# Gated attention and two expert products on one core: the gate applied as a square at the output, routing rows carrying logits and square sums

## The chip, the cores and the metric

The program runs on one NeuronCore of a Trainium2 chip. The metric is the device time of one execution in microseconds. Engines are named as in the profile: PE (TensorE, matrix products), PEld (its weight loads), DVE (VectorE), ACT (ScalarE), POOL (GpSimd) and SP (SyncE, which issues most DMAs). Each engine runs its own instructions in order; semaphores connect them.

## The reference

Three parts run one after the other, all in 32-bit floats:

```python
# 1. gated linear attention, 4 batches x 8 heads x 768 steps x 48 dims
f = sigmoid(f_logit)
for t in range(768):
    state = f[t][:, None] * state + outer(k[t], v[t])
    y[t] = q[t] @ state
x = y as 3072 tokens x 384
# 2. one of 8 experts for each token
logits = (x / |x|) @ (emb / |emb|).T / tau
e = argmax(logits); gate = softmax(logits)[e]
x = gate * (relu(x @ w1[e]) @ w2[e])          # 384 -> 1024 -> 384
# 3. a gated product for all tokens
out = ((x @ w_a) * (x @ w_b)) @ w_out         # 384 -> 1536 -> 384
```

The gate is a positive number for each token. Part 3 is quadratic in `x`, so a factor on a token's `x` comes out of it as its square.

## The kernel before

**Attention (about 0 to 150 us).** 24 groups: 6 chunks of 128 steps by 4 batches. The main loop over `g` issues the instructions of several groups in an order written by hand: `scan_b(g + 2)` and `scan_r(g + 2)` are the products of the gates as scans on VectorE (L197, L208); `scores(g + 1)` (L251) multiplies the scaled keys `kt`, made on GpSimd (L200), with the scaled queries `qc` (L216, VectorE); the masks follow (`mask_a` on ScalarE and GpSimd, `mask_v` on VectorE); `inter` and `intra` make the output, which `turn_y` (L316) turns to tokens by a product with `pick`. That product also gives each token's eight logits, because `pick` carries the expert embeddings divided by norm and `tau`. The norms are made in `names()` (L594 to L605), three pieces run in groups 0 and 1, with a power 0.5 on GpSimd (L599).

**Routing.** `ROUNDS` lists the groups at which a round closes: rounds of 8, 7, 3, 3 and 3 groups. `route` (L360) is a generator that the loop advances with `tick`: the norm of each token by a power on GpSimd (L373), maximum and one-hot on VectorE, ranks by small products on TensorE, a tanh on ScalarE for the exponentials, the softmax denominator `den` (L415 to L421), and the slot number `posi` (L412). `scatter_row` (L432) then writes 128 rows of 388 floats to `slots` in DRAM: 4 columns of head (number and denominator) and 384 of `x`. Each scatter is an indirect DMA on GpSimd's queue.

**The early half of expert 0.** At group 21 `early_load` reads the first 224 rows of expert 0, `early_gate` makes the rate (reciprocal of the denominator) and scales the rows by it on ScalarE (L460), `early_turn` turns them on TensorE (L467). `early_h`, `early_split` and `early_y` compute them while the last rounds are routed. Overflow flags and offsets follow on VectorE (L750 to L766).

**Experts (about 180 to 430 us).** 64 steps, 8 for each expert, 448 rows an expert. `rows_load` (L876) reads an expert's rows into the one buffer `rows`; `rows_rate` and `rows_gate` (L886, L892) scale them by the gate in place, on ScalarE (L896) after a rate on VectorE (L889, L890); `x_turn` (L915) turns them on TensorE and splits them in a high and a low part for products of full precision. Each step makes a hidden block (L932 to L934), splits it (`hh` on ScalarE L955, `hl` on VectorE L956) and multiplies it with the second weights (L989). `y_part` copies the finished expert into `yT` by ScalarE and VectorE (L1007, L1005). Loaded weights are split in two parts by `job_run` (L814): experts' weights in one ScalarE conversion (L817) and three subtractions (L820), the third part's weights, which are 64-bit words, by a longer VectorE chain (L828 to L838). `ids_store` keeps the token numbers in `idlist` in DRAM, in the order in which the rows stand in `yT`.

**Gated product (about 430 to 884 us).** 6 tiles of 512 tokens by 12 steps. `ab_part` makes the two products and multiplies them (L1088, L1092), splits the result in `gh` and `gl` (L1093, L1094), and `q_mm` multiplies with `w_out`, one step later. In the first ten steps the last wide weights are still split. `q_out` (L1111) copies 128 tokens of the result out and scatters them to the output by `idx`, made at L1057 from the list `idr` (L1050).

## Time and profile before

| | us |
|---|---|
| median of 3 runs | 891.82 (891.37 to 892.36) |
| profiled execution | 893.16 |
| its span | 891.4 |
| PE busy | 840.3 (94%) |
| DVE busy | 426.6 (48%) |
| ACT busy | 355.9 (40%) |
| POOL busy | 248.4 (28%) |

The span is what the profile covers; the profiled execution's own time holds 1.8 us more. Busy shares are means over stages with different limits. Matmuls overlap, so that a busy PE is not necessarily at its peak.

### The profile page before, as it was taken

What the parts mean: (1) busy time and instruction counts of PE and PEld (TensorE: products, weight loads), DVE (VectorE), ACT (ScalarE), POOL (GpSimd) and SP (SyncE); (2) the same over time, 40 slices, a digit from 0 to 9 for tenths busy, and PEclk for the clock granted to TensorE, in tenths of its full rate; (3) what the DMA queues carried; (4) which work ended last, traced back from release to release, by engine and by line L of the source; (5) the groups of instructions that cost most, each with busy time, mean ns of one, the idle gap of its engine ahead of it and who ended that gap; (6) DMA issues with size and microseconds to landing.
All of it is one profiled execution on the core that took longest, in us unless ns stands there. A gap on an engine that the chain in (4) does not pass through costs nothing. (4 is left out here: it accounts for less than half of the span.)

```text
span 891.4 us, 12984 instructions
## 1 busy us (share of the span) xinstructions
PE 840.3 (94%) x5149; PEld 742.5 (83%) x5149; DVE 426.6 (48%) x719; ACT 355.9 (40%) x681; POOL 248.4 (28%) x235
## 2 busy tenths in 40 slices
PE   6898987886999999999998999999999999999996
PEld 4787876875988898899887888888888888888885
DVE  8999995434354345447688523221322312222221
ACT  4798974343455445544443222121222212212111
POOL 6446865432634443461222110010010001001001
PEclk8899998988999999999999999999999999999998
DMA  9888851343534544442333000000000000000001
GB/s 188 207 213 204 242 161 71 111 133 102 174 111 145 198 141 138 139 145 73 103 107 107 1 36 1 1 36 0 1 27 10 1 1 35 1 1 36 1 1 39
DMA packets 35592, 76.60 MB, mean 86 GB/s; under 512 B 4604, under 2 KB 17428, under 8 KB 35524
## 3 DMA queue, kind: packets, MB, share of 16 engines
q1 hardware_dynamic: 32324, 65.91, 26.4%
q0 software_dynamic: 3072, 9.49, 2.9%
q8 instruction: 42, 0.69, 0.3%
q10 hardware_dynamic: 128, 0.30, 0.1%
q14 instruction: 26, 0.21, 0.1%
HBM read 63.79 MB, written 11.90 MB: 85 GB/s over the span
## 5 line engine op out<-in xcount | busy, mean ns | idle before, releaser
L934 PE MATMUL pa<-a,w 128*128 128x512 f32 (+1 forms) x438 | 170.7, 390 | 0.0
L933 PE MATMUL pa<-a,w 128*128 128x512 f32 (+1 forms) x438 | 170.5, 389 | 0.0
L932 PE MATMUL pa<-a,w 128*128 128x512 f32 (+1 forms) x438 | 169.2, 386 | 0.0
L1092 DVE TENSOR_TENSOR rows<-rows,pa 128x512 f32<-128x512 f32 (+1 forms) x73 | 49.6, 679 | 242.7 <-PE pa L934 242.7
L1119 POOL DMA_INDIRECT out<-yT,idx x24 | 23.5, 980 | 363.7 <-ACT yT L1117 358.2
L1088 ACT ACTIVATE rows<-pa 128x512 f32<-128x512 f32 (+1 forms) x73 | 43.1, 591 | 164.7 <-PE pa L934 164.4
L1093 ACT ACTIVATE gh<-rows 128x512 fp32r<-128x512 f32 (+1 forms) x73 | 45.6, 625 | 143.9 <-DVE rows L1092 143.9
L1107 PE MATMUL pq<-w,gl 128*128 128x384 f32 x288 | 97.6, 339 | 2.8 <-DVE gl L1094 2.6
L820 POOL TENSOR_TENSOR w<-raw,w 128x512 fp32r<-128x512 f32 x56 | 84.8, 1535 | 55.2 <-ACT w L817 50.7
L1105 PE MATMUL pq<-w,gh 128*128 128x384 f32 x288 | 97.2, 337 | 0.8 <-ACT gh L1093 0.8
L1106 PE MATMUL pq<-w,gh 128*128 128x384 f32 x288 | 96.9, 337 | 0.4 <-POOL w L838 0.4
L989 PE MATMUL po<-hh,w 128*128 128x448 f32 (+1 forms) x384 | 89.7, 365 | 6.9 <-ACT yT L1007 5.7
L934 PEld LDWEIGHTS pa<-a,w 128*128 128x128 f32 x438 | 82.3, 188 | 16.8
L933 PEld LDWEIGHTS pa<-a,w 128*128 128x128 f32 x438 | 82.3, 188 | 15.3
L932 PEld LDWEIGHTS pa<-a,w 128*128 128x128 f32 x438 | 82.4, 188 | 15.0
L1094 DVE TENSOR_TENSOR gl<-rows,gh 128x512 fp32r<-128x512 f32 (+1 forms) x73 | 60.0, 822 | 52.1 <-ACT gh L1093 52.1
L989 PEld LDWEIGHTS po<-hh,w 128*128 128x128 f32 x384 | 68.2, 191 | 15.0 <-ACT yT L1007 9.6
L838 POOL TENSOR_TENSOR w<-raw,w 128x768 fp32r<-128x768 f32 x18 | 33.9, 1881 | 144.0 <-ACT w L837 138.7
L955 ACT ACTIVATE hh<-ph 128x448 fp32r<-128x448 f32 (+1 forms) x64 | 33.3, 520 | 101.3 <-PE ph L934 101.2
L932 PE MATMUL ph<-a,w 128*128 128x448 f32 (+1 forms) x192 | 69.8, 363 | 0.1
L956 DVE SCALAR_TENSOR_TENSOR hl<-ph,hh 128x448 fp32r<-128x448 f32 (+1 forms) x64 | 38.0, 593 | 66.0 <-ACT hh L955 65.8
L933 PE MATMUL ph<-a,w 128*128 128x448 f32 (+1 forms) x192 | 69.3, 361 | 0.0
(202 smaller groups left out, 1432.9 us busy)
## 6 DMA issues: line engine op xcount, KB each, us to landing
raw<-moe_w SPq DMA_DIRECT2D x32, 768.0 KB, 4.7
qkf<-qkf SPq DMA_DIRECT2D x44, 288.0 KB, 6.0
rows<-slots SPq DMA_DIRECT2D x7, 679.0 KB, 6.6
vx<-vx SPq DMA_DIRECT2D x24, 192.0 KB, 4.1
raw<-moe_w_a SPq DMA_DIRECT2D x6, 768.0 KB, 4.4
raw<-moe_w_b SPq DMA_DIRECT2D x6, 768.0 KB, 4.7
raw<-moe_w_out SPq DMA_DIRECT2D x6, 768.0 KB, 4.3
slots<-raw SPq DMA_DIRECT2D x8, 291.0 KB, 4.3
```

What stands on the lines that cost most here:

```text
L820: (G if i < NPOOL else V).tensor_tensor(out=wt[:, 1, f], in0=raw[:, f], in1=wt[:, 0, f].bitcast(F32), op=ALU.subtract)
L932: T.matmul(out=out, lhsT=wh, rhs=xh, start=first, stop=False)
L933: T.matmul(out=out, lhsT=wl, rhs=xh, start=False, stop=False)
L934: T.matmul(out=out, lhsT=wh, rhs=xl, start=False, stop=last)
L989: T.matmul(out=OS[e][k], lhsT=w[:, j % 4, k * 128:(k + 1) * 128], rhs=x, start=(j == 0 and w is wh and x is hh), stop=(j == FJ - 1 and x i ...
L1088: A.activation(out=ab[:, r], in_=pa, func=ACTF.Copy)
L1092: V.tensor_tensor(out=ab[:, r], in0=ab[:, r], in1=pp[1], op=ALU.mult)
L1093: A.activation(out=gh[:, r], in_=ab[:, r], func=ACTF.Copy)
L1094: V.tensor_tensor(out=gl[:, r], in0=ab[:, r], in1=gh[:, r].bitcast(F32), op=ALU.subtract)
L1105: T.matmul(out=q, lhsT=gh[:, c], rhs=wh[:, f % 4], start=(f == 0), stop=False)
L1106: T.matmul(out=q, lhsT=gh[:, c], rhs=wl[:, f % 4], start=False, stop=False)
L1107: T.matmul(out=q, lhsT=gl[:, c], rhs=wh[:, f % 4], start=False, stop=(f == F2J - 1))
```

## The change

Rows are scattered ungated. Their head grows from 4 to 10 columns (`XO`, `RW`): token number, square sum, eight logits. ScalarE's square accumulates straight into the row, and the logits are reduced straight into it. `route` keeps only what the slot number needs. The token numbers of all groups are written once. The heads of an expert's rows go to `heads` in DRAM instead of the numbers to `idlist`; at step `IDS` they are read back with a token on each partition (`idf`), and in steps 1 to 6 of the gated product `gates` makes the square of the gate for all 3072 tokens at once. `q_out` multiplies by it.

Beside that: the rows of expert 1 have a buffer of their own (`rows1`, the tail of `yT[2]`) and are loaded with those of expert 0, those of expert 2 at step 0; the turning of rows stands in steps 3 to 5 for every expert; rounds are of 8, 6, 4, 3 and 3 groups; two scatters a group; the early load is at group 22; the embedding norms are made ahead of the loop; the conversions of weights 4 to 7 are cut in thirds over three steps. The core of the diff:

```diff
-ROUNDS = (7, 14, 17, 20, 23)
+ROUNDS = (7, 13, 17, 20, 23)
...
         def route(rd):
             nb = rd["n"]
-            lg, ssq = rd["lg"][:, 0:nb], rd["ssq"][:, 0:nb]
+            lg = rd["xb"][:, 0:nb, 2:XO]
...
-            nrm = rt("nrm", 1)
-            G.tensor_tensor(out=nrm[:, :, 0], in0=ssq, in1=half[:, 0:nb], op=ALU.pow)
-            G.tensor_scalar(out=nrm, in0=nrm, scalar1=1e-6, scalar2=None, op0=ALU.add)
-            yield
...
-            V.reciprocal(out=nrm, in_=nrm)
-            yield
-            V.tensor_tensor(out=z, in0=z, in1=bc(nrm), op=ALU.mult)
...
-            A.activation(out=z, in_=z, func=ACTF.Tanh, scale=0.5)
...
-            den = rt("den")
-            V.tensor_scalar(out=den, in0=z, scalar1=-1.0, scalar2=1.0, op0=ALU.mult, op1=ALU.add)
-            yield
-            V.reciprocal(out=den, in_=den)
-            yield
-            V.scalar_tensor_tensor(out=den, in0=z, scalar=1.0, in1=den, op0=ALU.add, op1=ALU.mult)
-            yield
-            V.tensor_reduce(out=rd["xb"][:, 0:nb, 1:2], in_=den, axis=AX.X, op=ALU.add)
...
+        en_ps = ps_r.tile([128, NE], F32, tag="r", name="en_ps")
+        A.activation(out=esq, in_=emb[0:HP], func=ACTF.Square)
...
         scores(0)
+        for p in range(NP):
+            T.matmul(out=en_ps, lhsT=onesf, rhs=esq[:, p], start=(p == 0), stop=(p == NP - 1))
+        A.activation(out=en, in_=en_ps, func=ACTF.Copy)
         turn_k(0)
         scan_b(1)
+        G.tensor_tensor(out=en, in0=en, in1=half[:, 0:NE], op=ALU.pow)
+        G.tensor_scalar(out=en, in0=en, scalar1=1e-6, scalar2=tau, op0=ALU.add, op1=ALU.mult)
...
-            if g == 21:
+            if g == 22:
                 early_load()
...
-            for _ in range(2 if g < 18 else 3):
+            for _ in range(2):
                 scatter_row()
...
             if g == 22:
-                early_gate()
                 w_lo(V, 2)
...
             if g in (20, 23):
-                for _ in range(3):
+                for _ in range(3 if g > 20 else 2):
                     scatter_row()
...
+        rows1 = yT[2][:, NT - 4 * RW:NT].rearrange("p (j w) -> p j w", j=4)
+        rows_of = lambda e: rows1 if e == 1 else rows
...
+            if c is None and n < 8:
+                for i in range(3):
+                    f = slice(i * 512, (i + 1) * 512)
+                    A.activation(out=wt[:, 0, f], in_=raw[:, f], func=ACTF.Copy)
+                    (G if i < NPOOL else V).tensor_tensor(out=wt[:, 1, f], in0=raw[:, f], in1=wt[:, 0, f].bitcast(F32),
+                                                          op=ALU.subtract)
+                    if i < 2:
+                        yield
+                return
...
             if s == 0:
-                rows_rate(0)
-                rows_gate(0, 2, V)
-                rows_gate(0, 3)
...
         rows_load(0)
+        rows_load(1)
         while wstate["load"] < 6:
             w_load()
...
             if s == 0:
                 ids_copy(0)
-                rows_load(1)
+                rows_load(2)
                 ids_store(0)
-            if j == late:
-                rows_rate(e + 1)
-            if late <= j < late + 2:
-                rows_gate(e + 1, 2 * (j - late))
-                rows_gate(e + 1, 2 * (j - late) + 1)
             w_more(s)
-            if late + 2 <= j < late + 5:
-                x_turn(e + 1, j - late - 2)
-            if j == late + 4:
+            if 3 <= j <= 5:
+                x_turn(e + 1, j - 3)
+            if j == 5:
                 ids_copy(e + 1)
-                rows_load(e + 2)
+                if e > 0:
+                    rows_load(e + 2)
...
             if s == IDS:
-                SP.dma_start(out=idr, in_=idlist[0, 0:NT].rearrange("(a b) -> a b", a=24))
+                SP.dma_start(out=idf, in_=heads[0:NT].rearrange("(t p) w -> p t w", p=128))
...
+        def gates():
+            nt = NT // 128
+            bc = lambda t: t.unsqueeze(2).to_broadcast([128, nt, NE])
+            lg = idf[:, :, 2:XO]
+            z, den, nrm, mx = gz[:, 0], gz[:, 1], gm[:, 0], gm[:, 1]
+            G.tensor_tensor(out=nrm, in0=idf[:, :, 1], in1=half, op=ALU.pow)
+            V.tensor_reduce(out=mx, in_=lg, axis=AX.X, op=ALU.max)
+            V.tensor_tensor(out=z, in0=lg, in1=bc(mx), op=ALU.subtract)
+            yield
+            yield
+            V.tensor_scalar(out=nrm, in0=nrm, scalar1=1e-6, scalar2=None, op0=ALU.add)
+            V.reciprocal(out=nrm, in_=nrm)
+            V.tensor_tensor(out=z, in0=z, in1=bc(nrm), op=ALU.mult)
+            A.activation(out=z, in_=z, func=ACTF.Tanh, scale=0.5)
+            yield
+            V.tensor_scalar(out=den, in0=z, scalar1=-1.0, scalar2=1.0, op0=ALU.mult, op1=ALU.add)
+            V.reciprocal(out=den, in_=den)
+            yield
+            V.scalar_tensor_tensor(out=den, in0=z, scalar=1.0, in1=den, op0=ALU.add, op1=ALU.mult)
+            V.tensor_reduce(out=g2, in_=den, axis=AX.X, op=ALU.add)
+            V.tensor_scalar(out=g2, in0=g2, scalar1=1e-9, scalar2=None, op0=ALU.add)
+            yield
+            V.reciprocal(out=g2, in_=g2)
+            V.tensor_tensor(out=g2, in0=g2, in1=g2, op=ALU.mult)
+            yield
...
             if i % 2:
-                V.tensor_copy(ob, QS[tt][i])
+                V.tensor_scalar(out=ob, in0=QS[tt][i], scalar1=sq, scalar2=None, op0=ALU.mult)
             else:
-                A.activation(out=ob, in_=QS[tt][i], func=ACTF.Copy)
+                A.activation(out=ob, in_=QS[tt][i], func=ACTF.Copy, scale=sq)
...
             q_part(s - 1)
+            if 1 <= s <= 6:
+                next(gate_ops)
             w_start(NE * FJ + s, 1)
```

## Rows read from the trace of the kernel before

**Rows 1.** Busy us by stage: span, PE, PEld, DVE, ACT, POOL; clock, DMA, GB/s:
```profile
26.00:142.00 116.00, 106.56 (x1351) 92.69 (x1350) 111.89 (x193) 95.96 (x253) 72.55 (x80) 0.96 0.75 197
180.00:205.00 25.00, 21.62 (x156) 20.13 (x157) 10.85 (x23) 13.22 (x23) 12.44 (x11) 0.87 0.37 101
205.00:224.00 19.00, 13.28 (x60) 11.87 (x59) 6.85 (x13) 6.92 (x12) 1.73 (x2) 0.82 0.33 109
437.00:503.50 66.50, 62.56 (x295) 53.47 (x295) 53.05 (x63) 25.46 (x39) 15.82 (x9) 1.00 0.26 84
```

**Rows 2.** Timeline of POOL, 67 to 146: start us, us, instruction [idle before <-releaser]:
```profile
67.74 2.56 POOL L373 TENSOR_TENSOR nrm<-ssq,half 128x8 f32<-128x8 f32 x1
...
142.69 0.97 POOL L435 DMA_INDIRECT slots<-xb,posi  x1 [0.30 <-issue]
143.67 1.20 POOL L200 TENSOR_TENSOR kt<-qkf,Bt 128x512 f32<-128x512 f32 x1
```

**Rows 3.** Timeline of PE, 144 to 216:
```profile
144.92 1.73 PE L251 MATMUL pp<-qc,kt 64*128 64x128 f32 x16 [3.83 <-POOL kt L200]
...
153.85 0.41 PE L467 MATMUL kv<-ident,rows 112*128 112x112 f32 x2
...
164.56 0.48 PE L496 MATMUL kv<-he,w 128*128 128x224 f32 x2 [1.13 <-DVE he L485]
...
180.68 0.98 PE L922 MATMUL pt<-ident,rows 112*128 112x112 f32 x4 [3.60 <-issue]
...
182.34 0.41 PE L934 MATMUL ph<-a,w 128*128 128x224 f32 x1
...
215.29 1.11 PE L989 MATMUL po<-hh,w 128*128 128x448 f32 x2 [5.72 <-ACT yT L1007]
```

**Rows 4.** Timeline of DVE, 163 to 213:
```profile
163.81 0.17 DVE L391 RECIPROCAL nrm<-nrm 128x3 f32<-128x3 f32 x1 [3.38 <-POOL nrm L374]
...
179.70 0.14 DVE L766 CAST flag_b<-flag_i 1x1 bf16<-1x1 int32 x1
...
212.69 0.17 DVE L889 TENSOR_SCALAR rg<-rows 112x4 f32<-112x4 f32 x1 [4.89 <-DMA rows<-slots]
```

**Rows 5.** Timeline of ACT, 212 to 216:
```profile
213.10 1.12 ACT L896 ACTIVATE rows<-rows,rg 112x384 f32<-112x384 f32 x2 [5.97 <-DVE rg L890]
```

**Rows 6.** Timeline of DVE, 420 to 453:
```profile
423.62 0.18 DVE L1057 SCALAR_TENSOR_TENSOR idx<-fl_sb,pt 128x24 int32<-128x24 f32 x1
...
434.08 0.69 DVE L1094 TENSOR_TENSOR gl<-rows,gh 128x512 fp32r<-128x512 f32 x1 [0.70 <-ACT gh L1093]
...
452.48 1.95 DVE L1094 TENSOR_TENSOR gl<-rows,gh 128x512 fp32r<-128x512 f32 x1 [0.90 <-ACT gh L1093]
```

**Rows 7.** Timeline of DVE, 22 to 80:
```profile
23.00 2.10 DVE L601 TENSOR_SCALAR en<-en,tau 128x8 f32<-128x8 f32 x1 [0.17 <-POOL en L599]
...
25.48 1.23 DVE L208 TENSOR_TENSOR_SCAN Rt<-F,patr 128x516 f32<-128x516 f32 x1
...
68.90 0.69 DVE L216 TENSOR_TENSOR qc<-qkf,Rt 128x512 f32<-128x512 f32 x1
...
70.68 0.20 DVE L391 RECIPROCAL nrm<-nrm 128x8 f32<-128x8 f32 x1
...
71.06 1.23 DVE L197 TENSOR_TENSOR_SCAN Bt<-F,pat 128x516 f32<-128x516 f32 x1
...
76.34 0.18 DVE L415 TENSOR_SCALAR den<-z 128x64 f32<-128x64 f32 x1
76.56 0.55 DVE L417 RECIPROCAL den<-den 128x64 f32<-128x64 f32 x1
...
77.54 0.26 DVE L426 TENSOR_REDUCE new<-oh 128x8 f32<-128x64 bf16 x1
```

**Rows 8.** Timeline of SP's queue, 404 to 415:
```profile
404.78 0.38 SPq L1050 DMA_DIRECT2D idr<-idlist  x1
```

**Rows 9.** Part 3 of the page: packets, MB, share of 16 engines:
```profile
q1 hardware_dynamic: 32324, 65.91, 26.4%
```

More of the change, by code (lines that the diff above doesn't have):

```diff
@@ L25 @@
 CAP = 448
-RW = 388
+RW = 394
 SROWS = NE * NT
@@ L35 @@
 RB = 8
-XO = 4
+XO = 10
 NQ = 4
@@ L72, in build @@
     rows = epool.tile([128, 4, RW], F32, name="rows")
-    rg = epool.tile([HP, 4], F32, name="rg")
-    ids0 = epool.tile([HP, 2], F32, name="ids0")
-    eo = epool.tile([128, KC, EN], F32, name="eo")
+    eo = rows[:, 0:2].rearrange("p a b -> p (a b)")[:, 0:KC * EN].rearrange("p (k n) -> p k n", k=KC)
+    ids0 = epool.tile([HP, 2, XO], F32, name="ids0")
+    half = epool.tile([128, NT // 128], F32, name="half")
     pieces = []
@@ L353, in x_lg @@
                 bg.append(route(rd))
-                next(bg[-1])
         scat = []
@@ L452, in early_load @@
                     mybir.DependencyClass.Sync, mybir.DependencyReason.DATA), reason="rows arrived")
-        def early_gate():
-            V.tensor_scalar(out=rg[:, 0:2], in0=rows[0:HP, 0:2, 1], scalar1=1e-9, scalar2=None, op0=ALU.add)
-            V.reciprocal(out=rg[:, 0:2], in_=rg[:, 0:2])
-            V.tensor_copy(ids0, rows[0:HP, 0:2, 0])
-            for j in range(2):
-                r = rows[0:HP, j, XO:RW]
-                A.activation(out=r, in_=r, func=ACTF.Copy, scale=rg[:, j:j + 1])
         def early_turn():
+            V.tensor_copy(ids0, rows[0:HP, 0:2, 0:XO])
             kv = ps_k.tile([128, 512], F32, tag="kv", name="kv")
@@ L533, in build @@
         load_a(0, (SP, A), True)
-        V.memset(half, 0.5)
+        V.memset(half[:, 0:NE], 0.5)
         V.memset(ones, 1.0)
         V.memset(warm, 0.0)
-        A.activation(out=half, in_=half, func=ACTF.Tanh, scale=0.0, bias=0.0)
+        A.activation(out=half[:, 0:NE], in_=half[:, 0:NE], func=ACTF.Tanh, scale=0.0, bias=0.0)
         clear(1, V, V, V)
         load_a(1, (SP, SP), True)
+        SP.dma_start(out=emb, in_=I["embp"])
+        tau = ob_p.tile([128, 1], F32, name="tau")
+        SP.dma_start(out=tau, in_=I["tau"].to_broadcast([128, 1]))
         load_b(0)
@@ L561, in build @@
         gate_f(0)
-        SP.dma_start(out=emb, in_=I["embp"])
-        tau = ob_p.tile([128, 1], F32, name="tau")
-        SP.dma_start(out=tau, in_=I["tau"].to_broadcast([128, 1]))
         load_a(3)
@@ L590, in build @@
         q_scale(1)
-        en_ps = ps_r.tile([128, NP, NE], F32, tag="r", name="en_ps")
-        en = ob_p.tile([128, NE], F32, name="en")
-        def names():
-            V.tensor_tensor(out=esq, in0=fl(emb)[0:HP], in1=fl(emb)[0:HP], op=ALU.mult)
-            T.matmul(out=en_ps, lhsT=onesf, rhs=esq, start=True, stop=True)
-            yield
-            V.tensor_reduce(out=en, in_=en_ps.rearrange("p h e -> p e h"), axis=AX.X, op=ALU.add)
-            G.tensor_tensor(out=en, in0=en, in1=half, op=ALU.pow)
-            yield
-            V.tensor_scalar(out=en, in0=en, scalar1=1e-6, scalar2=tau, op0=ALU.add, op1=ALU.mult)
-            V.reciprocal(out=en, in_=en)
-            V.tensor_tensor(out=pick[:, :, 2 * D:XW], in0=emb, in1=en.unsqueeze(1).to_broadcast([128, NP, NE]),
-                            op=ALU.mult)
-            yield
-        setup = names()
         def zero_fill(i):
@@ L619, in build @@
             if g == 3:
-                SP.dma_start(out=idlist[0].rearrange("(p a) -> p a", p=80), in_=zero[0:80, 0:(NT + CAP) // 80])
+                SP.dma_start(out=heads.rearrange("(p a) w -> p (a w)", p=110), in_=zero[0:110, 0:(NT + CAP) * XO // 110])
             if 3 <= g < NE + 3:
@@ L641, in build @@
                 al_keep((g + 2) // B)
-            if g == 1:
-                next(setup)
+            if g == 0:
+                V.reciprocal(out=en, in_=en)
+                V.tensor_tensor(out=pick[:, :, 2 * D:XW], in0=emb, in1=en.unsqueeze(1).to_broadcast([128, NP, NE]),
+                                op=ALU.mult)
             inter(g)
@@ L709, in build @@
         early_y(0)
-        tick(1)
+        tick(2)
+        for _ in range(3):
+            scatter_row()
+        tick(3)
         early_h(2)
-        tick(2)
         early_split(2)
@@ L715, in build @@
         early_h(3)
-        tick(4)
-        for _ in range(3):
-            scatter_row()
-        tick(3)
         early_split(3)
@@ L879, in rows_load @@
                 src = slots[e * NT + at:e * NT + CAP].rearrange("(p j) w -> p j w", p=HP)
-                ld = SP.dma_start(out=rows[0:HP, 2 if e == 0 else 0:4], in_=src).ins
+                ld = SP.dma_start(out=rows_of(e)[0:HP, 2 if e == 0 else 0:4], in_=src).ins
                 for sc in scat:
@@ L921, in x_turn @@
             for j in range(n):
-                T.transpose(pt[:, j], rows[0:HP, 4 - n + j, XO + k * 128:XO + (k + 1) * 128], ident[:HP, :HP])
+                T.transpose(pt[:, j], rows_of(e)[0:HP, 4 - n + j, XO + k * 128:XO + (k + 1) * 128], ident[:HP, :HP])
             src = pt.rearrange("p j a -> p a j")
```

77 lines of the change are left out of this document (28 added, 49 removed).

## The prediction

> **What bounds the kernel now.** I read the busy table by stages first, then the waits of TensorE, then the timelines of the engines around each of its gaps. From about 224 us on TensorE is busy without a gap, so nothing that the change takes from VectorE, ScalarE or GpSimd there can show, with one exception below. The time lies in earlier places.
>
> In the attention loop (26 to 142 us) VectorE is busy 111.89 of 116 us and TensorE 106.56 [rows 1]: VectorE's order of instructions is the path, so an instruction taken from it there shortens the loop by its own duration. At the end of that loop GpSimd takes over: TensorE waits 3.83 us for `kt` of the last group, which stands on GpSimd's queue behind four row scatters, the last of them at 142.69 [rows 2, 3]. At the change of stage TensorE stands 3.60 us (to 180.68) with the chain of the overflow flags and the gate on VectorE in front of it [rows 3, 4]. At 215.29 it comes back from the longest wait, 5.72 us, for ScalarE's copy L1007 [rows 3]. That copy stands behind two gate scalings (L896) that had waited 5.97 us for the rate, and the rate had waited 4.89 us for the rows of expert 2, loaded late into the only row buffer [rows 4, 5]. The granted clock falls with these gaps: 0.87 and 0.82 as means over 180 to 205 and 205 to 224 us [rows 1], so a gap costs its length and some matmuls at the lower of the two levels after it.
>
> The exception is 437 to 503.5 us: at full clock TensorE is busy 62.56 of 66.5 us, VectorE 53.05 [rows 1]. Each step there has a serial chain: wide weight work on VectorE, then its halves on ScalarE and GpSimd, then `gl` on VectorE, which takes 1.95 us instead of 0.69 when GpSimd subtracts beside it [rows 6]. The chain is longer than TensorE's step, and work added to VectorE there is paid in full. The change adds its gates exactly there.
>
> **Part by part.** Gains are positive; all are from the profiled execution.
>
> *The embedding norms (start).* Squares go to ScalarE, the sum over heads into TensorE's accumulation, `tau` scaling to GpSimd, the power ahead of the loop. VectorE loses L601, which held it from 22.83 to 25.10 with its wait [rows 7], and two operations of about 0.2 us; the reciprocal and the product remain and stand earlier. That is 2.6 us for the scan L208 that now starts at 25.48 [rows 7]. A later wait of VectorE for TensorE shrinks too, because TensorE no longer stands before the first logits. Against this, ScalarE waits for the embedding before it clears two accumulators, GpSimd's power delays the first mask, and two small loads stand ahead of others on SP's queue; these I see beside waits for loads that the start has anyway. I take +3.0, bounds -0.5 (all of it lost to the prologue) and +4.
>
> *Gate work out of the routing.* Per round VectorE loses the reciprocal and product of the norm (70.68 to 71.06) and four operations from `den` on (76.34 to 77.54): 0.38 + 1.20 = 1.58 us for the round of eight groups [rows 7]. The second round has six groups instead of seven, about 1.5. Of the third only the first two operations count here, 0.3. Sum +3.4, bounds 2.5 and 4; GpSimd's powers (2.56 us for eight columns) [rows 2] leave as well, but they did not hold VectorE. ScalarE's small tanh is off the path.
>
> *The end of the loop.* After the second round of six groups no scatter is left over when the third is ready, and two instead of four stand ahead of the last `kt`. A scatter costs 0.97 us [rows 2] and some issue time; with the three operations saved before it, `kt` starts some 3.5 us earlier relative to the rest and is no longer late. What is late next is the early load of rows: it now stands one group later and waits for the two scatters behind `kt`. By my count its rows land 1.4 us after TensorE asks for them, against a transpose at 153.85 (L467) that had a gate before it [rows 3]. Net +4.3, bounds 2.0 and 5.0.
>
> *The early half of expert 0.* VectorE waited 3.38 us for the last power [rows 4], which TensorE felt as 1.13 us [rows 3]; I add 0.5 for the shorter routing before it. +1.6, bounds 0.5 and 1.8.
>
> *The change of stage.* Rows of expert 0 need no rate and no scaling, so the transposes go as soon as TensorE is through. What is late next is the flag chain on VectorE, which ends at 179.84 [rows 4] and precedes the low halves of the transposed rows. First low half at 179.84 + 0.4 = 180.2 instead of just before 182.34 [rows 3]: +2.0, bounds 0.5 and 4 (the clock stays up).
>
> *Expert 0 in the main loop.* In 180 to 205 us TensorE is idle 3.4 us and partly at the lower level [rows 1]: 0.13 x 25 = 3.3 us of clock. The waits come from gates before the transposes and from unbroken conversions on ScalarE in front of `hh`. The gates go, the first four weight conversions are cut in thirds. But the load of expert 1's rows now goes into the tail of `yT`, memory of the closed stage, and stands on SP's queue ahead of the weight loads 4 and 5; if that memory is given free only with the flag chain, weight 4 arrives some 2 us after ScalarE reaches it. +3.5, bounds 0 and 5.9.
>
> *Expert 1.* Rows of expert 2 are asked for about 20 us earlier (step 0 instead of step 6), and no gate stands before the copy L1007. The 5.72 us go [rows 3], and about 2.5 of the 0.18 x 19 = 3.4 us that the clock lost in 205 to 224 [rows 1]. +8.2, bounds 5.5 and 8.7.
>
> *Gates in the second product.* Twelve VectorE operations in steps 1 to 6. Six on 192 columns, between 0.18 (24 columns, L1057) and three times 0.26 (64 columns, L426): I take 0.35 each, 2.1. One reciprocal of 192 columns, three times L417's 0.55 less its fixed part: 1.35 [rows 6, 7]. Five on 24 columns at 0.2: 1.0. Together 4.45. Besides, ScalarE's tanh waits for VectorE and holds back the opening operation of the wide job queued behind it, on which VectorE waits: I take 1.2. GpSimd's power of 24 columns, an estimate of 6.7 us from 2.56 for eight [rows 2], delays a weight half by some 0.6. Less 0.7 of slack in step 2: -5.5, bounds -8 and -2.5.
>
> GpSimd's power against VectorE: the operation `qc` with two inputs from SBUF took 0.69 us at 68.90, in the middle of the power of 67.74 to 70.30 [rows 2, 7], so the power did not hold it, while the subtraction on GpSimd does stretch `gl` [rows 6]. The Trainium skill (SBUF — State Buffer, "Who interferes with whom") says that a VectorE instruction with two SBUF inputs and a GpSimd instruction that reads SBUF exclude each other for a whole instruction. By that rule the long power would block `gl` too; the trace agrees for the subtraction and not for the power, and the sum goes by the trace.
>
> *At nothing:* scaling in the output copies (same element count; last two on the end, within 0.2); rows 1.5% wider, hidden with a transfer share of 0.75 at most in the loop [rows 1]; one row-number fill instead of 24 on GpSimd; wider `heads` stores beside full TensorE work; and the list read back at the end in 3072 pieces of 40 bytes instead of 24. That read was issued at 404.78 and its user ran at 423.62 [rows 6, 8]: 18.8 us of cover. Each of 16 engines gets 192 pieces. Queue 1's packets took 26.4% of 16 engines over 891.4 us for 32324 packets, 0.116 us each at 2 KB [rows 9]; at that price 22 us, 3.5 too late; as nearly all of a 2 KB packet is data I take half or less, 11 us, covered.
>
> **Sum.** 3.0 + 3.4 + 4.3 + 1.6 + 2.0 + 3.5 + 8.2 - 5.5 = 20.5 us. 893.16 (the profiled execution: span 891.4 and 1.8 around it) becomes 872.7; it lies 1.3 over the median of the runs, 891.82, which becomes **871.3**.
>
> **Rivals.**
> - *The new load blocks SP's queue.* The two terms at the change of stage shrink from 5.5 to 1: 876. For it: the load is now the first to use memory that tiles of the closed stage held, and SP's queue is in order; against: weights 4 and 5 are needed only by expert 1. 0.17.
> - *GpSimd's long power excludes VectorE.* Its 6.7 us come to the chain in step 1 to 2, less 0.9 of slack: 877. The `qc` row speaks against it. 0.07.
> - *The wait before 215 us isn't the gate's doing* and returns as a wait for another copy on ScalarE: 8.2 lost, 880. The order of rows speaks against it. 0.06.
> - *Clock.* With shorter gaps it stays up everywhere; 7 more: 864. 0.08.
> - *The other side: the 40-byte read.* All rests on 18.8 us of cover. If a piece costs more than 0.21 us, 192 of them take 40 us and the index, with VectorE's whole queue behind it, is late by the full gain; at 0.25 us they take 48, 29 us late: 900. For it: no row has such pieces. Against: 0.116 us with fifty times the data. 0.05. The Trainium skill (DMA: Bandwidth & Descriptors, "Specifications") names 512 bytes as the least transfer at full rate, with a read-modify-write below it; no row here shows that.
>
> My forecast holds 0.57; its own range is 866 to 877. Eight times in ten I expect 862 to 882, which takes in the first three rivals and the gain bounds. Differences under 0.2% can't be told from none here. Faster 0.93, same 0.02, slower 0.05.
>
> **What would show it.** Right: no wait of TensorE over 2 us between 130 and 230 us; the last attention scan about 10 us earlier; TensorE's gap at the change of stage under 2 us; granted clock over 0.9 in each 20 us after 150; TensorE idle 9 to 10 us instead of 3.9 in the second product's first ten steps [rows 1]. Wrong: ScalarE waiting for weight 4 over 3 us, VectorE waiting for the read-back list, or the loop of 26 to 142 us unchanged in length, which would mean that VectorE was not its bound.

## The result and the profile after

| | before | after |
|---|---|---|
| median, us | 892.09 (891.37 to 894.26, 4 runs) | 878.37 (878.03 to 878.86, 4 runs) |
| profiled execution, its span | 893.16, 891.4 | 878.86, 876.8 |

The ratio is 0.9843 (95% interval 0.9824 to 0.9861): 13.7 us faster where 20.5 were forecast. 878.4 us lies in the range of 862 to 882 that took in the rivals, and outside the 866 to 877 that the prediction gave to its own account. Here is where the span's 14.6 us came from, by marks that both kernels have. Each number is the start of one instruction in the timelines.

| mark | before | after | gain so far | forecast so far |
|---|---|---|---|---|
| fourth masked product (DVE `pm<-pp`) | 31.05 | 28.07 | 3.0 | 3.0 |
| last attention scan (DVE `Bt`) | 138.34 | 130.32 | 8.0 | 6.4 |
| `kt` of the last group (POOL) | 143.67 | 134.39 | 9.3 | |
| early rows transposed (PE) | 153.85 | 144.53 | 9.3 | 10.7 |
| early accumulators copied (ACT) | 177.00 | 168.27 | 8.7 | 12.3 |
| first `hl` of the expert steps (DVE) | 186.12 | 175.80 | 10.3 | 14.3 |
| expert 0 copied to `yT` (ACT) | 214.9 | 193.16 | 21.7 | |
| first `gl` of the second product (DVE) | 434.08 | 411.18 | 22.9 | 26.0 |
| its twelfth `gl` | 507.0 | 489.5 | 17.5 | 20.5 |
| its last `gl` | 880.27 | 865.00 | 15.3 | 20.5 |
| end of the span | 891.4 | 876.8 | 14.6 | 20.5 |

The busy table of the changed kernel, over the stretches that answer to [rows 1] (span, PE, PEld, DVE, ACT, POOL, granted clock, DMA share, GB/s):

```profile
26.00:134.00 108.00, 100.23 (x1322) 87.26 (x1318) 105.13 (x175) 92.96 (x246) 65.41 (x58) 0.99 0.81 214
171.20:193.00 21.80, 21.43 (x168) 21.03 (x168) 9.06 (x20) 11.20 (x26) 10.29 (x10) 0.92 0.76 217
193.00:215.00 22.00, 22.00 (x117) 20.24 (x116) 11.06 (x18) 8.69 (x16) 6.24 (x5) 1.00 0.36 110
414.10:485.90 71.80, 63.98 (x296) 53.20 (x295) 57.00 (x75) 25.50 (x39) 19.90 (x10) 1.00 0.24 77
```

Read the last line against the last of [rows 1], which holds the same ten steps: TensorE does the same work, but the stretch is 5.3 us longer and its idle time is 7.8 us instead of 3.9. The third line has no gap and full clock where before there were 5.72 us of wait. TensorE's own timeline of the changed kernel shows what took the place of the gaps of [rows 3] (start, duration, instruction, wait before it):

```profile
144.53 0.41 PE L433 MATMUL kv<-ident,rows 112*128 112x112 f32 x2 [1.72 <-DMA rows<-slots]
...
171.57 0.37 PE L884 MATMUL ph<-a,w 128*128 128x224 f32 x1 [2.84 <-ACT a L877]
```

The second of them is a new wait. ScalarE's timeline, and the SP queue's, name what it stands for:

```profile
171.16 0.61 ACT L877 ACTIVATE a<-pt 128x224 fp32r<-128x224 f32 x2 [2.29 <-DVE flag_b L718]
```
```profile
171.12 0.30 SPq L846 DMA_DIRECT2D yT<-slots  x1
171.47 0.95 SPq L102 DMA_DIRECT2D raw<-moe_w  x2
```

A copy of transposed rows waits for the last flag operation, with which it shares no data. The trace shows the wait; that its target `a` lies in memory of the closed stage is read from the code. The loads of expert 1's rows and of weights 4 and 5 are let go at the same moment.

### The profile page after: what moved, and what is told of

The parts are those of the page before. It is cut to its first block, busy times and chain, and to the rows that moved or that the text cites. A ratio compares the mean times of both kernels' runs of the same rounds, so it can differ in the third digit from the quotient of the medians.

```text
span 876.8 us, 12913 instructions
## 1 busy us (share of the span) xinstructions
PE 838.9 (96%) x5154; PEld 739.4 (84%) x5154; DVE 422.9 (48%) x680; ACT 341.9 (39%) x656; POOL 243.2 (28%) x204
## 3 DMA queue, kind: packets, MB, share of 16 engines
q0 software_dynamic: 3072, 9.56, 3.1%
## 4 chain that ended last, share of the span: by engine, by line
issue 50%; PE 32%; DVE 7%; POOL 6%; DMA 3%; ACT 1%; POOLq 0%; SPq 0%; ACTq 0%; DVEq 0%
PE po L938 11%; PE ph L884 4%; PE ph L886 4%; PE ph L885 4%; POOL out L1091 2%; POOL w L804 2%; DVE Rt L206 2%; PE pp L249 2%; DMA qkf<-qkf 2%; PE x_ps L314 1%; PE y_ps L273 1%; PE y_ps L280 1%; DVE qc L214 1%; PE pt L874 1%; DVE pm L266 1%
## 5 line engine op out<-in xcount | busy, mean ns | idle before, releaser
L938 PE MATMUL po<-hh,w 128*128 128x448 f32 (+1 forms) x384 | 86.9, 361 | 1.0 <-ACT yT L956 1.0
L786 POOL TENSOR_TENSOR w<-raw,w 128x512 fp32r<-128x512 f32 x48 | 72.9, 1540 | 41.4 <-ACT w L783 41.4
## 6 DMA issues: line engine op xcount, KB each, us to landing
vx<-vx SPq DMA_DIRECT2D x24, 192.0 KB
```

The lines of the kernel that those rows point to most:

```text
L786: (G if i < NPOOL else V).tensor_tensor(out=wt[:, 1, f], in0=raw[:, f], in1=wt[:, 0, f].bitcast(F32), op=ALU.subtract)
L938: T.matmul(out=OS[e][k], lhsT=w[:, j % 4, k * 128:(k + 1) * 128], rhs=x, start=(j == 0 and w is wh and x is hh), stop=(j == FJ - 1 and x i ...
```

## The experiments

All are edits of the changed kernel unless said otherwise. Times differ by some 0.2 to 0.3% from run to run, so below that the marks of the traces decide. Each ratio is to runs of the kernel before that were taken with it. By the ratios alone the paddings, the flag chain, the swapped order and the rounds can't be told from each other.

| run | median, us | ratio to before, 95% interval |
|---|---|---|
| gates in steps 8 to 11 | 873.21 | 0.9762 (0.9726 to 0.9797) |
| 32 bytes of padding | 875.95 | 0.9795 (0.9766 to 0.9823) |
| 416 bytes of padding | 874.63 | 0.9800 (0.9771 to 0.9830) |
| flag chain earlier | 876.51 | 0.9798 (0.9768 to 0.9828) |
| the same, weight 4 later | 874.86 | 0.9795 (0.9775 to 0.9815) |
| `x` product ahead of early transposes | 877.87 | 0.9815 (0.9795 to 0.9835) |
| round closed after group 14 | 877.46 | 0.9814 (0.9794 to 0.9835) |
| the same, with GpSimd's powers | 879.51 | 0.9839 (0.9807 to 0.9871) |
| old start | 879.14 | 0.9847 (0.9830 to 0.9863) |
| before, without main gate scaling | 885.84 | 0.9914 (0.9882 to 0.9945) |
| before again | 893.73 | 0.9995 (0.9981 to 1.0009) |
| combined | 856.56 | 0.9592 (0.9576 to 0.9608) |

### Gates later in the second product

```diff
-            if 1 <= s <= 6:
-                next(gate_ops)
+            for _ in range((0, 1, 1, 2, 2)[max(0, s - 7)] if s < 12 else 0):
+                next(gate_ops)
```

> The changed kernel with its gate operations run in steps 8 to 11 of the second product instead of 1 to 6. Theory (the gate's twelve VectorE operations lengthen a chain that is already longer than TensorE's step while the wide weights are made): the 5.4 us that the changed kernel lost between steps 2 and 9 come back but for some 0.7 us of the two operations that still fall into step 8, so 878.4 becomes 873.7; TensorE's waits for gl fall from 5.8 to about 3 us. Rival (the second product begins 22.9 us earlier, and the wide weights' own loads and conversions are late for it, whatever the gates do): no change, 878.4.

873.21 us. From the first `gl` to the twelfth it takes 73.6 us, against 78.3 in the changed kernel and 72.9 before. TensorE's waits there (engine, line, releaser: us in total, times, longest), first in the changed kernel, then here:

```profile
PE pq L1050 <- DVE gl L1037: 5.8, 5, 1.4
PE pq L1048 <- ACT gh L1036: 1.6, 2, 1.2
```
```profile
PE pq L1050 <- DVE gl L1037: 2.5, 3, 1.3
PE pq L1048 <- ACT gh L1036: 0.8, 1, 0.8
```

The price is the gates' place and not their size: VectorE still does all of them, in steps where it has time. The rival falls.

### Two paddings for the slow steps of the second product

From the twelfth `gl` on nothing waits in either kernel, yet the changed one takes 375.5 us to the last `gl` and the one before 373.3. The steps differ by their weights. Three stretches of four steps each, `gl` of steps 35, 39, 43 and 47, in the kernel before and then after:

```profile
656.41 0.69 DVE L1094 TENSOR_TENSOR gl<-rows,gh 128x512 fp32r<-128x512 f32 x1 [0.70 <-ACT gh L1093]
...
681.32 0.69 DVE L1094 TENSOR_TENSOR gl<-rows,gh 128x512 fp32r<-128x512 f32 x1 [0.70 <-ACT gh L1093]
...
706.22 0.69 DVE L1094 TENSOR_TENSOR gl<-rows,gh 128x512 fp32r<-128x512 f32 x1 [0.70 <-ACT gh L1093]
...
731.13 0.69 DVE L1094 TENSOR_TENSOR gl<-rows,gh 128x512 fp32r<-128x512 f32 x1 [0.70 <-ACT gh L1093]
```
```profile
639.82 0.69 DVE L1037 TENSOR_TENSOR gl<-rows,gh 128x512 fp32r<-128x512 f32 x1 [0.70 <-ACT gh L1036]
...
664.69 0.69 DVE L1037 TENSOR_TENSOR gl<-rows,gh 128x512 fp32r<-128x512 f32 x1 [0.70 <-ACT gh L1036]
...
689.92 0.69 DVE L1037 TENSOR_TENSOR gl<-rows,gh 128x512 fp32r<-128x512 f32 x1 [0.70 <-ACT gh L1036]
...
715.00 0.69 DVE L1037 TENSOR_TENSOR gl<-rows,gh 128x512 fp32r<-128x512 f32 x1 [0.70 <-ACT gh L1036]
```

Before, four steps take 24.9 us whatever their weights. After, they take 24.87, 25.23 and 25.08. Their `pa` weights lie in tiles 6 and 7, then 2 and 3, then 0 and 5: tiles 0 to 3 are the ring allocated ahead of the attention stage, and the steps are slower the more of it they use. The two edits, each a run of its own:

```diff
+    shift = epool.tile([128, 8], F32, name="shift")      # 32 bytes a partition
+    shift = epool.tile([128, 104], F32, name="shift")    # 416 bytes
```

> The changed kernel with one unused tile of 32 bytes per partition, which moves the tiles allocated after it (activations, weights 4 to 8, hidden halves, outputs) by 32 bytes, to the place within 64 bytes that they had before. Theory (the steps of the second product take 6.267 us instead of 6.228 because of where its tiles lie): steps of 6.23 again, 2.2 us less, 876.2. Rival (the pace differs from execution to execution or from chip to chip): steps of 6.27 and 878.4.

> The changed kernel with one unused tile of 416 bytes per partition ahead of the stage's tiles. In the second product the steps with weights from tiles 6 and 7 take 6.22 us in both kernels, those with weights from the older ring (tiles 0 to 3) 6.23 before and 6.27 to 6.31 after; only these were moved against the activations (104800 bytes between tile 2 and the activations instead of 107264, a multiple of 256). The 416 bytes make it 105216, a multiple of 256 again. Theory (the distance between the weights and the moving operand decides): all steps 6.23, 2.2 us less, 876.2. Rival (something else slows these steps): still 6.27 to 6.31, 878.4.

With 32 bytes the steps stay slow (375.4 us from the twelfth to the last `gl`); with 416 they take what they took before (373.3), as the four rows of that run show:

```profile
637.77 0.69 DVE L1038 TENSOR_TENSOR gl<-rows,gh 128x512 fp32r<-128x512 f32 x1 [0.70 <-ACT gh L1037]
...
662.67 0.69 DVE L1038 TENSOR_TENSOR gl<-rows,gh 128x512 fp32r<-128x512 f32 x1 [0.70 <-ACT gh L1037]
...
687.58 0.69 DVE L1038 TENSOR_TENSOR gl<-rows,gh 128x512 fp32r<-128x512 f32 x1 [0.70 <-ACT gh L1037]
...
712.49 0.69 DVE L1038 TENSOR_TENSOR gl<-rows,gh 128x512 fp32r<-128x512 f32 x1 [0.70 <-ACT gh L1037]
```

So the place of the weights against the activations decides these 2.2 us, or against the hidden halves and outputs that the padding moves along with them. The medians don't show it: the run with 32 bytes, whose steps stayed slow, is 2.4 us under the changed kernel too. Which residue matters is open: 107264 and 105216 bytes were fast, 104800 and 104832 slow, and 256 is one divisor among several that the fast ones share.

### The flag chain earlier, then weight 4 later

```diff
         early_split(6)
+        V.tensor_copy(cnt_sb, pc[0:1, 0, 0:NE])
...
+        V.tensor_tensor(out=off_i, in0=off_f[:, 0], in1=off_f[:, 3], op=ALU.min)
         early_y(5)
...
         early_split(7)
+        V.tensor_reduce(out=fl2[:, 0:1], in_=cnt_sb, axis=AX.X, op=ALU.max)
...
+        V.tensor_copy(flag_b, flag_i)
         early_y(6)
```

> The changed kernel with the chain of the overflow flags on VectorE run six operations behind the low half of early step 6 and eight behind that of step 7, instead of all behind the early accumulators' copies. Theory (memory of the closed stage is given free only when that chain ends, and the first copy of the transposed rows waits for it, 2.84 us of TensorE): first low-half product 2.6 us earlier against the stage before, about 1 us more from the clock, 878.4 becomes 874.8. Rival (something else of that stage holds the memory or the rows, as the early accumulators' copy on GpSimd): the wait stays and the time is 878.4; a second rival is that the chain now delays the low half of early step 7 and TensorE waits there instead, 877.5.

The wait for `a` fell from 2.84 to 0.5 us and the first `hl` came at 172.4 instead of 175.8. But expert 0 was copied at 192.0, only 1.2 us earlier than in the changed kernel. ScalarE's timeline shows who took the rest:

```profile
177.62 0.63 ACT L776 ACTIVATE w<-raw 128x512 fp32r<-128x512 f32 x1 [4.91 <-DMA raw<-moe_w]
```

The conversion of weight 4 waits for its load, and the copies of hidden steps 2 and 3 stand behind it. So the second run starts that conversion at step 2:

```diff
-        loaded.extend((-9, n, None, RAW[n]) for n in (4, 5))
+        loaded.extend((0, n, None, RAW[n]) for n in (4, 5))
```

> The flag chain moved up as in the earlier run, and the first conversion of weight 4 on ScalarE put off from step 0 to step 2 of expert 0. Theory (of the 3.4 us that the moved chain gained, 2.2 were lost because ScalarE stood 4.91 us for weight 4's load, with the copies of hidden step 2 behind it): the gain stays, 875.0 in the median. Rival (the loads themselves are the bound, and the later weights are late instead): 876.5 as in the earlier run or worse.

874.86 us. Between 165 and 235 us TensorE has one wait of 0.5 us left. From the copy of the early accumulators to the first `gl` it takes 238.4 us, against 242.9 in the changed kernel. Weight 4 was the second wait behind the first.

### TensorE's order in the early half

```diff
-            if g == NG - 1:
-                early_turn()
             if g > 0:
                 turn_y(g - 1)
+            if g == NG - 1:
+                early_turn()
```

> The changed kernel with the transposes of the early rows queued behind the last but one group's x product on TensorE instead of ahead of it. Theory (the early half lost against the forecast because TensorE stands 1.7 us for rows at 144.5 and then runs 6 us at the lower clock): 1.1 us of that product fill the wait, 0.6 us of wait stays, 877.0; if the clock stays up with it, 875. Rival (the transposed halves on ScalarE and VectorE are late for the first early step instead): no change, 878.4.

The wait for rows went and the clock stayed up. 145 to 150 us in the changed kernel, then here (columns as in the busy table):

```profile
145.00:150.00 5.00, 4.19 (x21) 4.19 (x21) 2.47 (x9) 1.63 (x5) 0.98 (x1) 0.50 0.00 0
```
```profile
145.00:150.00 5.00, 4.03 (x35) 3.65 (x35) 2.69 (x12) 2.64 (x10) 0.57 (x1) 1.00 0.00 0
```

Yet the time did not change beyond what can be told (877.87). The early steps began 1.8 us sooner (150.6 against 152.4), and ended no sooner (168.5 against 168.3): TensorE waited 0.9 us for `he` on ScalarE and 1.1 for a weight half on VectorE. ScalarE's timeline shows what stands ahead of both waits:

```profile
155.16 0.36 ACT L450 ACTIVATE he<-u_ps 128x224 fp32r<-128x224 f32 x1 [4.18 <-remote]
```

ScalarE stood still for 4.18 us, and the trace names no engine for it. In the ten other profiles of the changed kernel and its versions this copy starts 2.4 to 2.7 us after the one before it, here 4.55. Whether the pause belongs to the new order or to this one execution, the slowest of the four (880.82; the others 875.88 to 878.12), stays open. So this run doesn't say what the lost clock is worth.

Five other profiles do. From TensorE's first transpose of the early rows to ScalarE's first `he` stands the same work in all of them:

| kernel | wait for rows, us | first transpose to first `he`, us | clock there | first `he` to the copy of the accumulators, us |
|---|---|---|---|---|
| before | none | 4.88 | 1.00 | 18.27 |
| changed | 1.72 | 7.50 | 0.54 | 16.24 |
| old start (below) | 1.86 | 6.35 | 0.73 | 16.24 |
| GpSimd's powers (below) | none | 4.88 | 1.00 | 16.40 |
| combined (below) | none | 4.88 | 1.00 | 16.42 |

The lower clock behind the wait costs the changed kernel 2.6 us, and where it stays up they come back. ScalarE's first `he` before, then after; the busy table of the two stretches, in the same order:

```profile
158.73 0.36 ACT L484 ACTIVATE he<-u_ps 128x224 fp32r<-128x224 f32 x1 [0.38 <-PE u_ps L480]
```
```profile
152.03 0.36 ACT L450 ACTIVATE he<-u_ps 128x224 fp32r<-128x224 f32 x1 [1.13 <-PE u_ps L446]
```
```profile
153.80:158.80 5.00, 3.97 (x38) 3.71 (x35) 2.90 (x13) 2.80 (x10) 0.00 (x0) 1.00 0.00 0
```
```profile
144.50:152.00 7.50, 6.60 (x33) 6.39 (x34) 3.58 (x15) 2.23 (x7) 2.57 (x3) 0.54 0.13 46
```

### The end of the loop: rounds, or GpSimd's powers

```diff
-ROUNDS = (7, 13, 17, 20, 23)
+ROUNDS = (7, 14, 17, 20, 23)
```

> The changed kernel with the second round of routing after group 14 again, as before (rounds of 8, 7, 3, 3, 3 groups instead of 8, 6, 4, 3, 3). Theory (the term for the end of the loop: rows left over stand ahead of the last kt on GpSimd): TensorE waits some 3 us for kt again, the early rows are loaded later, 878.4 becomes 882.0. Rival (the routing is now short enough that no row is left over either way): a wait under 1 us for kt, 878.4 to 879.

877.46 us; the theory falls. Four scatters stood ahead of the last `kt` as before the change, and `kt` still came 4.1 us behind the last scan. In the changed kernel, with two scatters ahead of it, that is 4.1 too: the first of them waited for the routing, and both took longer than the 0.97 us that the forecast counted:

```profile
130.37 2.00 POOL L408 DMA_INDIRECT slots<-xb,posi  x1 [1.15 <-DVE new L399]
132.67 1.70 POOL L408 DMA_INDIRECT slots<-xb,posi  x1 [0.30 <-issue]
134.39 1.19 POOL L198 TENSOR_TENSOR kt<-qkf,Bt 128x512 f32<-128x512 f32 x1
...
137.65 1.98 POOL L408 DMA_INDIRECT slots<-xb,posi  x1 [0.30 <-issue]
```

The second run has this edit and the powers of the routing too:

```diff
+            nrm = rt("nrm", 1)
+            G.tensor_tensor(out=nrm[:, :, 0], in0=rd["xb"][:, 0:nb, 1], in1=half[:, 0:nb], op=ALU.pow)
+            G.tensor_scalar(out=nrm, in0=nrm, scalar1=1e-6, scalar2=None, op0=ALU.add)
             mx = rt("mx", 1)
```

> The run with the second round after group 14, and with GpSimd's power and addition put back at the head of each routing round as before (their result is not used). Round 14 alone left kt of the last group where the changed kernel has it (134.6 us, 4.0 behind the last attention scan, before 5.3) and cost nothing. Theory (GpSimd's powers, 2 to 2.6 us a round, held the scatters and with them kt): kt comes 1.5 to 3 us later again, TensorE waits 3 us for it, 879 to 880. Rival (VectorE's shorter rounds alone brought kt forward): kt within 0.5 us of 134.6 plus the start, 877.5.

GpSimd's timeline of that run; a power stands in front of `kt`, and the scatters behind it are late:

```profile
125.78 1.44 POOL L365 TENSOR_TENSOR nrm<-xb,half 128x3 f32<-128x3 f32 x1
127.31 0.24 POOL L366 TENSOR_SCALAR nrm<-nrm 128x3 f32<-128x3 f32 x1
127.63 1.19 POOL L198 TENSOR_TENSOR kt<-qkf,Bt 128x512 f32<-128x512 f32 x1
...
136.73 1.21 POOL L198 TENSOR_TENSOR kt<-qkf,Bt 128x512 f32<-128x512 f32 x1
```

`kt` is 5.3 us behind the last scan again, and TensorE waits 2.7 us for it (1.4 without the powers). So the powers made it late, as the theory said. It cost less than the wait: the early steps begin at 153.0 instead of 152.7, because rows that arrive while TensorE waits for `kt` are not waited for later and the clock stays at 1.00 behind them, and the first `hl` comes at 176.2 us as without the powers (176.1). The median is 2.0 us up, which is no more than runs differ by; the last `gl` comes 0.9 later.

### The gate scaling taken out of the kernel before

```diff
-            if j == late:
-                rows_rate(e + 1)
-            if late <= j < late + 2:
-                rows_gate(e + 1, 2 * (j - late))
-                rows_gate(e + 1, 2 * (j - late) + 1)
```

> The kernel before, without the rate and the scaling of the rows of experts 1 to 7 (that part of the gate is left out of the result); rows of expert 2 are still loaded late into the only buffer. Theory (the wait of 5.72 us at 215 us is the gate scaling standing in front of ScalarE's copies): the wait goes, with it 2.5 us of slow clock, 891.9 becomes 883.7. Rival (the late rows themselves are the cause): a wait of 4 to 6 us of TensorE comes back at expert 2's transposes or at the copies, and the time is 890 to 892.

The wait of 5.72 us is gone, though the rows of expert 2 are loaded as late as before; that is the theory's part. From the first `hl` to the first `gl` it takes 242.3 us instead of 248.0, so it is worth 5.7 and not 8.2: a wait for another ScalarE copy grew from 0.8 to 3.1. The rest of the run's 7.5 us lies at its start (the fourth masked product at 28.9), which the edit doesn't touch.

### The start

The kernel before was profiled again, unchanged, and the changed kernel was given the old start: `names()` as before, its three pieces run in groups 0 and 1, and the squares and the power ahead of the loop taken out.

```diff
-        A.activation(out=esq, in_=emb[0:HP], func=ACTF.Square)
...
-        G.tensor_tensor(out=en, in0=en, in1=half[:, 0:NE], op=ALU.pow)
-        G.tensor_scalar(out=en, in0=en, scalar1=1e-6, scalar2=tau, op0=ALU.add, op1=ALU.mult)
...
+        setup = names()
...
+            if g == 1:
+                next(setup)
...
+            if g == 0:
+                next(setup)
+                next(setup)
```

> The kernel before, unchanged, for a second profile of it. The fourth masked product (DVE pm<-pp, the mark for the end of the start) stood at 31.05 in its first profile and at 28.86 in the run without gates, whose start is the same code; there the operation L601 took 0.22 us instead of 2.10. Theory (the 2.10 us belong to one execution, an overlap with GpSimd's kt that comes and goes): the mark lies at 28 to 30 and the span at 889 to 890. Rival (the start of the kernel before is as its first profile shows): 31, span 891.

> The changed kernel with the embedding norms as they were before (squares on VectorE, sum over heads on VectorE, power inside the loop, embedding and tau loaded behind the first groups). Forecast's term (+3.0 for that part): 881.4, the mark of the fourth masked product at 31. Theory now (the term rested on 2.10 us of L601 that not every execution has; without them the two orders differ by under 1 us): 878.4 to 879.4, the mark at 28.5 to 29.5. Rival on the other side (the new order's own costs, GpSimd's power before the first mask, are larger than what it saves): 877.5.

L601 in the second profile of before, and the same operation in the changed kernel with the old start:

```profile
22.90 2.10 DVE L601 TENSOR_SCALAR en<-en,tau 128x8 f32<-128x8 f32 x1 [0.17 <-POOL en L599]
```
```profile
24.33 0.47 DVE L567 TENSOR_SCALAR en<-en,tau 128x8 f32<-128x8 f32 x1
```

The rival was right on this second profile: 2.10 us again, and the mark at 30.9. But the run without gates, with the same start, had 0.22 us and 28.9, so two of three profiles of this start have the 2.10 us and one doesn't. In the changed kernel the old start puts the mark at 29.2, where ten profiles of versions with the new start have it between 27.1 and 29.4, and the last `gl` comes at 865.1 instead of 865.0. Against the changed kernel the mark is 1.1 us later; the first `he` is not (152.0 in both), because the clock fell less behind the wait for rows (the table above). Undone alone, the new start is worth nothing that can be told.

### The findings together

Gates late, 416 bytes, flag chain earlier, weight 4 later, and a fifth edit in the chain of the wide steps:

```diff
             A.activation(out=hi, in_=as3(r0), func=ACTF.Copy)
-            G.tensor_tensor(out=lo, in0=as3(r0), in1=hi.bitcast(F32), op=ALU.subtract)
+            if len(GS):
+                yield
+            (V if len(GS) else G).tensor_tensor(out=lo, in0=as3(r0), in1=hi.bitcast(F32), op=ALU.subtract)
...
-                            job_load(s)
                 V.tensor_tensor(out=ab[:, r], in0=ab[:, r], in1=pp[1], op=ALU.mult)
+                if at == 0:
+                    w_next()
+                    job_load(s)
```

> The changed kernel with what the runs pointed to: gates in steps 8 to 11 of the second product (-5.2), weights and activations a multiple of 256 bytes apart (-2.2 to -3.7), flag chain moved up and weight 4 converted two steps later (-3.5); and, new, the low half of the wide weights subtracted on VectorE between the product and gl instead of on GpSimd beside gl. Theory (that subtraction stretches gl from 0.69 to 1.95 us; on VectorE it takes 0.96 and falls into the 0.9 us in which VectorE waits for gh): the chain of a wide step goes from 7.2 to about 6.3 us, some 4 us less over eight steps, in all 863. Rival (VectorE is the bound and the 0.96 us are paid in full): 867.

856.56 us, 4.1% under before and some 2.5% under the changed kernel. VectorE's timeline of one wide step, where `gl` took 1.95 us in [rows 6], and the busy table of ten steps:

```profile
417.56 0.69 DVE L1037 TENSOR_TENSOR rows<-rows,pa 128x512 f32<-128x512 f32 x1 [0.22 <-PE pa L889]
418.32 0.96 DVE L807 TENSOR_TENSOR w<-raw,w 128x768 fp32r<-128x768 f32 x1
419.20 0.69 DVE L1042 TENSOR_TENSOR gl<-rows,gh 128x512 fp32r<-128x512 f32 x1
```
```profile
404.50:472.30 67.80, 67.80 (x329) 59.77 (x328) 56.12 (x85) 28.74 (x42) 0.00 (x0) 1.00 0.26 82
```

From the first `gl` to the twelfth it takes 67.2 us, and TensorE has no gap there. That is 6.5 under the run with late gates alone, more than expected. The early half gave some 2.4 us that were not counted: from TensorE's first transpose of the early rows to the copy of the accumulators it takes 21.3 us instead of 23.7, TensorE waits for no rows, and the clock is 1.00 from 140 us on. The rows came in time because the second scatter behind `kt`, the last that their load waits for, took 0.97 us here instead of 1.98, so that the load was issued 6.0 us after `kt` started instead of 7.0:

```profile
136.80 0.97 POOL L409 DMA_INDIRECT slots<-xb,posi  x1 [0.30 <-issue]
```

No edit touches these instructions. In eight of the eleven profiles of the changed kernel and its versions that scatter starts within 0.3 us after VectorE began to subtract a weight half (137.56 in the changed kernel), takes 1.8 to 2.0 us, and TensorE waits for the rows. In the other three (swapped order, GpSimd's powers, combined) it starts 0.3 to 0.7 us ahead of that subtraction, takes 1.0, and TensorE doesn't wait. So these 2.4 us hang on less than a microsecond in the order of the two engines, and no run moved the subtraction by itself.

## Why the prediction was right in direction and 6 us too high

Points in the order of the sum; measured values are differences between the marks above.

- **The loop and its end: 9.3 us at the early transposes, 10.7 forecast.** Two misses stand against each other here. The loop, from the fourth masked product to the last scan, gave 5.0 us where 3.4 were forecast; where the other 1.6 come from is not tested. From the last scan to the early transposes it was 1.3 instead of 4.3, the largest single miss. `kt` came 4.1 us behind the last scan instead of 5.3, so 1.3 sooner and not 3.5. The step that gave this gain to fewer scatters ahead of `kt` is refuted by round 14. What gave the 1.3 was the going of GpSimd's powers, as their return showed (5.3 again). The step "they did not hold VectorE" holds, since the loop kept its 5.0 us with the powers back; that they counted for nothing was too narrow, as they held the scatters and `kt`. The start's 3.0 were right as a difference of the two profiles, but undoing it alone costs nothing at the end.
- **The early half of expert 0: -0.6 instead of +1.6. This step failed.** Its own gain came: from the first `he` to the copy of the accumulators the time fell by 2.0 us. The forecast put the rows 1.4 us behind TensorE's request (1.72 measured) and counted that wait, but not what follows it: clock 0.54 from the first transpose to the first `he`, 2.6 us more than at full clock.
- **The change of stage: 1.6, forecast 2.0.** The flag chain was named as the next limit, which was right. How it limits was not: not by VectorE's place alone, for ScalarE's first copy waited for its last operation (171.0), and two loads were let go with it.
- **Experts 0 and 1 in the main loop: 12.6, forecast 11.7.** The wait of 5.72 us was the gate's doing, as the run without gate scaling shows; the 2.5 us of clock went with it, and the stretch from 193 to 215 us runs at 1.00. The sum came out better than its parts: the gate scaling alone was worth 5.7 of the 8.2 in the kernel before, so if the parts add, 6.9 are left where 3.5 were forecast for expert 0. No run separates them, and that the two misses cancel is luck.
- **Gates in the second product: -5.4, forecast -5.5.** The twelve operations took 4.5 us (4.45 estimated) and came on a chain that was already the longer one. GpSimd's power of 24 columns took 4.2 us instead of 6.7.
- **Not in the sum: -2.2 for the placement of weights against activations, and -0.7 at the end,** where the last scatter's landing took 7.0 us of the span instead of 6.4. Nothing in the diff's operations points to the first.

So the misses are 1.4 (3.0 less 1.6), 2.2 and 0.4 us in the stages before 186 us, 0.9 and 0.1 the other way behind them, and 2.9 unforeseen: 5.9 of the 20.5, which leaves the 14.6 of the span.

Of the rivals, the new load on SP's queue was half right: nothing at the change of stage was lost to it as long as the flag chain was later, and it showed as weight 4's 4.91 us once the chain was gone. The 40-byte read cost nothing: issued at 380.08, its pieces had moved by 384, at 0.011 us apiece (from 380 to 384 us the 16 engines were 52.5% busy with 3088 pieces), far from the 0.21 at which it would have mattered.

On GpSimd's power the sum went by the trace, and the changed kernel bears that out. GpSimd's timeline, a subtraction and the power, then VectorE's: a conversion step beside the subtraction, two operations inside the power, and `gl` beside a later subtraction:

```profile
404.35 1.88 POOL L804 TENSOR_TENSOR w<-raw,w 128x768 fp32r<-128x768 f32 x1 [5.81 <-ACT w L803]
...
414.82 4.22 POOL L1059 TENSOR_TENSOR gm<-idf,half 128x24 f32<-128x24 f32 x1
```
```profile
405.08 1.56 DVE L795 TENSOR_SCALAR ct<-ct 128x768 f32<-128x768 f32 x1 [0.94 <-ACT ct L794]
...
417.29 0.36 DVE L1061 TENSOR_TENSOR gz<-idf,gm 128x192 f32<-128x192 f32 x1
417.57 0.55 DVE L795 TENSOR_SCALAR ct<-ct 128x768 f32<-128x768 f32 x1
...
422.92 1.96 DVE L1037 TENSOR_TENSOR gl<-rows,gh 128x512 fp32r<-128x512 f32 x1 [0.96 <-ACT gh L1036]
```

Inside the power an operation with two inputs in SBUF ran in 0.36 us, and a conversion step in 0.55, which took 1.56 beside the subtraction. `gl` took 1.96 beside the subtraction that starts at 422.44. The Trainium skill (SBUF — State Buffer, "Who interferes with whom") lets both exclude VectorE; the trace agrees for the subtraction only.

Of the signs that the prediction named, two failed (a wait of 2.84 us between 130 and 230, and with it the gap at the change of stage), two came out smaller (the last scan 8.0 us earlier instead of about 10, though the terms of the sum ahead of it make 6.4; TensorE idle 7.8 us in the second product's first ten steps instead of 9 to 10), and one held (a clock over 0.9 in each 20 us after 150).

## What to carry to other kernels

A gain upstream is only worth what the next late thing leaves of it: behind the flag chain stood weight 4's load, and a wait that is removed should be priced together with its successor. A new wait costs its length and, where the clock falls behind it, more: 1.72 us of wait for rows brought 2.6 us of lower clock. Work moved "to where engines are idle" belongs where the serial chain has slack in that very step: the same twelve operations cost some 5 us in steps 1 to 6 and under 1 us in steps 8 to 11. Before a tile changes its size, look at what its new size moves.

## What the runs showed of the hardware

- The pace of products in full precision depends on where the weights lie against the moving operand: 6.23 us a step at a distance of 107264 or 105216 bytes, 6.27 to 6.31 at 104800 or 104832, with no wait in the trace. The Trainium skill (SBUF — State Buffer, "Who interferes with whom") gives TensorE independent read ports for the moving operand and the weights; by that alone the distance would not matter, and these runs differ from it.
- Where GpSimd's subtraction had begun first, it stretched VectorE operations that work on SBUF alone, also one with a single input: conversion steps (L795) took 1.55 us instead of 0.55 beside it, while `hl`, which reads PSUM, kept its 0.62.
- After a wait of 1.72 us TensorE ran at clock 0.50 from 145 to 150 us, its lower level of 1.2 GHz, in the changed kernel; in the run with the swapped order, without that wait, it ran at 1.00. In the run with the old start a wait of 1.86 us left 0.79 in the same 5 us.
- A row scatter on GpSimd's queue took 0.97 or 0.98 us where it started ahead of VectorE's weight subtraction and 1.8 to 2.0 where it started inside it (the second scatter behind the last `kt`, eleven profiles).
